# Recurrent attention and a feed-forward block on one core: second products held back, scores of a unit in one run over four PSUM banks, longer table phases

## The chip, the cores and the metric

The kernel runs on one core of a Trainium2 chip. The metric is the device time of one execution in microseconds (us). Before the change the median of 12 runs is 187.29 us (186.58 to 189.39).

## The reference

Only what is computed matters here:

```python
# q, k, v, f_logit: (4, 8, 768, 48)   (batch, heads, time, head width)
f = 1 / (1 + exp(-f_logit))
for t in range(S):
    state = f[:, :, t, :, None] * state + einsum('bhd,bhe->bhde', k[:, :, t], v[:, :, t])
    y[:, :, t] = einsum('bhd,bhde->bhe', q[:, :, t], state)
x = y.transpose(0, 2, 1, 3).reshape(3072, 384)
h = x @ w_in                                    # 384 x 2048
out = (0.5 * h * (1 + erf(h / sqrt(2)))) @ w_out   # 2048 x 384
```

The first half is a recurrence with a decay per channel; the second is a feed-forward block with an exact gelu.

## The kernel before, in words

Time is cut into chunks of 128 steps: 4 batches x 6 chunks = 24 chunks, handled as 12 units of two. The recurrence over a chunk becomes matrix products. For a unit, `decays` takes exp and ln of the forget logits on ScalarE (lines 456 and 459), sums the logarithms over time on TensorE (477 to 482 or 472 to 474, "sums"), and takes exp of the sums both ways, rg (487) and gt (489), and of the chunk's whole decay, gl (492, 496). VectorE multiplies k by rg and q by gt into sc (502, called kp and qp); v is cast to bf16 (507). `turn` transposes sc into kq: for units 0 to 4 on TensorE (535) with a copy out of PSUM (541), for units 5 to 11 by a transposing DMA on SP's queue (523). Then come the scores of a chunk, four pairs of heads, two half-height matmuls at a time (638, or 687 for units 0 to 4, whose rows are interleaved, "paired"), which fill two PSUM banks; VectorE masks them (548) into am. The state is carried by a product on TensorE (648, 699), an addition on VectorE (572), a multiplication (574) and two casts (579) on POOL. The output is the sum of an inner product (661, 719, called Y or YI) and one with the state (616, 622, YX), copied to yb (592) and transposed to xT, on TensorE with a copy for units 0 to 2 (608, 611), else by DMA.

`ffn_group` then takes a unit's 256 rows. Eight first products (755), each of six matmuls into one PSUM bank, are each followed by a gelu on ScalarE (765) into gT. For each of the two chunks 16 second products (774), four in an operation, accumulate in one bank; VectorE copies the bank to osb (788) and SP stores it. The words "first products" and "second products" below mean these.

The order is not written by hand. Every operation is put in a list with its engine, a fixed duration, what it reads and writes, its buffers and a priority; `Plan.run` (line 111 on) places them one after another by a small list scheduler: the operation that can start earliest on its engine, rounded to 0.05 us, then the lowest priority. The instructions are issued in that order, so every engine's order is fixed when the program is built. Exp with ln and gelu live in different tables of ScalarE. When the next operation needs the other table, its start is put off by up to `PATIENCE`; the table load itself is written at line 816. Filler matmuls (811) keep TensorE at work in the first 30 us. Banks are pooled: in `BANKS` five belong to first and second products (`s_fh`), three to attention (`s_m`, `s_ap`).

The order of the loads is the list `LOADS`: u0 stands for the four tensors of unit 0 (f_logit, k, q, v, in the kernel fl, kt, qt, vt), i0 to i2 for the pieces of w_in (win; 1024, 512 and 512 columns), o0 to o3 for those of w_out (wout). Inputs go through SP's queue, weights through POOL's, with a cast. Where the list changes from one queue to the other, a load waits for an earlier one of the other queue (function `load`).

```python
x = max(t, min(t + 2 * TABLE, max([d.vis for d in o.deps] + [switched]) + PATIENCE))
key = (int((x - (EAGER if o.eng == "PE" and o.prio < 900 else 0.0)) * 20 + 0.999), o.prio, o.seq)
```

Of the kernel before, what the change touches and what calls it, by code (L numbers as in the profile page):

```python
# [10 lines left out]
BF16 = mybir.dt.bfloat16  # L11
# [5 lines left out]
LAT = {"PE": 0.25, "ACT": 0.16, "DVE": 0.14, "POOL": 0.12, "DMA": 1.0}  # L17
TABLE = 1.28

PATIENCE = 1.0  # L20

SHARED = 0.5

TURN = 0.1

SPREAD, SEED = (0.0, 0)

EAGER = 0.0
PRI = {'C': 0, 'T': 1, 'A': 2, 'S': 2.5, 'Y': 3, 'X': 4, 'F': 5}
BANKS = (5, 0, 3)  # L30


class Slots:
# [34 lines left out]

class Op:
    __slots__ = ("eng", "dur", "fn", "bufs", "prio", "deps", "table", "start", "end", "vis", "seq", "name",  # L70
                 "left", "outs", "inst", "chain", "opens", "lag", "lat", "port", "mode")


class Plan:
# [3 lines left out]
    def __init__(self):  # L78
        self.ops, self.w, self.r = [], {}, {}

    def add(self, eng, dur, fn, rd=(), wr=(), bufs=(), prio=0.0, deps=(), table=None, name="", chain=None, opens=None, lag=0.0, lat=None, port=False, mode=0):
        o = Op()
        o.eng, o.dur, o.fn, o.bufs, o.prio, o.table, o.name = eng, dur, fn, tuple(bufs), prio, table, name
        o.start = o.end = o.vis = o.inst = None
        o.chain, o.opens, o.lag, o.port, o.mode = chain, opens, lag, port or eng == "POOL", mode
        o.lat = LAT[eng] if lat is None else lat
        o.seq = len(self.ops)
        d = list(deps) + ([chain] if chain else [])
        for k in rd:
            d += self.w.get(k, [])  # L90
        for k in wr:
            d += self.w.get(k, []) + self.r.get(k, [])
        for k in rd:
            self.r.setdefault(k, []).append(o)
        for k in wr:
            self.w[k] = [o]
            self.r[k] = []
        o.deps = list({id(x): x for x in d if x is not o}.values())
        for b in o.bufs:
            b.users.append(o)  # L100
        self.ops.append(o)
        return o

    def run(self):
# [6 lines left out]
        act, switched, mode = None, 0.0, 0  # L111
# [9 lines left out]
        while ready:  # L121
            best = None
            for o in ready:
                t = free[o.eng]
                for d in o.deps:
                    v = d.end if d.eng == o.eng and (o.eng != "DMA" or d is o.chain) else d.vis + o.lag
                    t = v if v > t else t
                ok, taken = True, {}
                for b in o.bufs:
                    if b.slot is None:  # L130
                        v, k = b.slots.free(), taken.get(id(b.slots), 0)
                        if len(v) <= k:
                            ok = False
                            break
                        t = max(t, v[k][0])
                        taken[id(b.slots)] = k + 1
                if not ok:
                    continue
                x = t
                if o.table and act and o.table != act:  # L140
                    x = max(t, min(t + 2 * TABLE, max([d.vis for d in o.deps] + [switched]) + PATIENCE))
                key = (int((x - (EAGER if o.eng == "PE" and o.prio < 900 else 0.0)) * 20 + 0.999), o.prio, o.seq)
                if best is None or key < best[0]:
                    best = (key, t, o)
            if best is None:
                raise RuntimeError("no operation can be placed: %s" % [o.name for o in ready[:20]])
            _, t, o = best
            d = o.dur
            if o.eng == "PE" and o.mode != mode:
                mode = o.mode  # L150
                d += TURN
            if o.port:
                other = port["POOL" if o.eng == "DVE" else "DVE"]
                d += SHARED * max(0.0, min(other[1], t + d) - max(other[0], t))
            if o.table and o.table != act:
                act, switched = o.table, t
# [12 lines left out]
            for n in o.outs:  # L169
                n.left -= 1  # L170
                if not n.left:
                    ready.append(n)
# [17 lines left out]
SIZES = [2, 2, 2, 2, 2, 2, 2, 2, 2, 2, 2, 2]  # L190
PAIRS = [0, 1, 2, 3, 4]
WIN = [1024, 512, 512]
EG = [1]
ET = [0, 1]
EX = [0]
EA = [0, 1]
SPLIT = []
HVC = [0, 1]
HKQ = [0, 2, 4]
HYB = [1]  # L200
HX = []
GKP, GQP = ([], [])
GAM = []
ODVE = [0, 1, 2, 3, 4, 5, 6, 7, 8, 9, 10, 11, 12, 13, 14, 15, 16, 17, 18, 19, 20, 21, 22, 23]
XDMA = [3, 4, 5, 6, 7, 8, 9, 10, 11]
KDMA = [5, 6, 7, 8, 9, 10, 11]
WARM = 30.0
LOADS = ['u0', 'u1', 'i0', 'i1', 'i2', 'o0', 'o1', 'u2', 'o2', 'o3']
LOADS += [f"u{n}" for n in range(12) if f"u{n}" not in LOADS and f"c{2 * n}" not in LOADS]


@with_exitstack
def kernel(
# [59 lines left out]
    s_yb = slots(3, [C, 2, HD], BF16, "yb")  # L273
    s_os = slots(4, [C, d_model], F32, "osb")
    s_xT = {s: slots({1: 4, 2: 4}.get(s, 2), [C, s, KO, C], BF16, f"xT{s}") for s in set(SIZES)}
    s_gT = {s: slots({1: 4, 2: 4}.get(s, 2), [C, FO, s * C], BF16, f"gT{s}") for s in set(SIZES)}
    banks = [pp.tile([C, 512], F32, name=f"ps{i}") for i in range(8)]
    nf, na, _ = BANKS
    s_fh, s_m = Slots(nf, banks[:nf]), Slots(8 - nf - na, banks[nf + na:])
# [115 lines left out]
    wo_src = moe_w_out.rearrange("(r p j) m -> r p j m", r=4, j=4)  # L395
    for what in LOADS:
        m = int(what[1:])
        if what[0] in "uc":
            js = (0, 1)
            if what[0] == "c":  # L400
                js, m = (m % 2,), m // 2
            x = U[m]
            names = (("fl", f_logit), ("kt", k), ("qt", q), ("vt", v))
            if x["pair"]:
                assert what[0] == "u"
                for nm, a in names:
                    if nm == "fl" and m in SPLIT:
                        for i in range(2):
                            load("sp", lambda x=x, a=a, m=m, i=i: nc.sync.dma_start(
                                out=x["fl"].t().rearrange("p (h x) -> p h x", h=H)[:, 4 * i:4 * i + 4], in_=srcp(a, m)[:, 4 * i:4 * i + 4]),  # L410
                                [("fl", 2 * m + i)], [x[nm]], 0.85, f"fl{m}.{i}")
                        continue
# [3 lines left out]
            else:  # L416
                for j in js:
                    for nm, a in names:
                        load("sp", lambda x=x, nm=nm, a=a, m=m, j=j: nc.sync.dma_start(
                            out=half(m, x[nm], j), in_=src(a, 2 * m + j)),  # L420
                            [(nm, 2 * m + j)], [x[nm]], 1.05, f"{nm}{m}.{j}")
        elif what[0] == "i" and m < len(WIN):
            load("pool", lambda m=m: nc.gpsimd.dma_start(out=win[m], in_=win_src[:, :, wcol[m]:wcol[m] + WIN[m]]),
                 [f"win{m}"], [], {512: 2.56, 1024: 4.4}[WIN[m]], what)
        elif what[0] == "o":
            load("pool", lambda m=m: nc.gpsimd.dma_start(out=wout[m], in_=wo_src[m]), [f"wout{m}"], [], 2.15, what)

# [197 lines left out]
    def attn_nat(u):  # L625
        kq = s_kq.new()
        turn(u, kq)
        for j in range(2):
            n = 2 * u + j
            c, x, pr = n % nC, X[n], 10 * n  # L630
            sc, vb = x["sc"], x["vb"]
            aps, ams = [s_ap.new(), s_ap.new()], [s_am.new(), s_am.new()]

            def amm(j=j, aps=aps):
                for p in range(P2):
                    for hh in range(2):
                        r = slice(64 * hh, 64 * hh + 64)
                        nc.tensor.matmul(aps[hh].t()[:, p * C:(p + 1) * C], kq.t()[r, 0, p, j, :], kq.t()[r, 1, p, j, :],  # L638
                                         start=True, stop=True)
            P.add("PE", 0.23, amm, mode=1, rd=[("kq", n)], wr=[("ap", n)], bufs=[kq] + aps + ams, prio=pr + PRI["A"], opens=aps[0], name=f"A{n}")  # L640
            mask_scores(aps, ams, ("am", n), f"AM{n}", ("ap", n), pr, mask, "mask")
            osb = St.get("sb") if c else None
            if c < nC - 1:
                sp = s_m.new()
# [24 lines left out]
    def attn_pair(u):  # L669
# [4 lines left out]
        pr = 10 * n0  # L674
        vbs, scs = [X[n]["vb"] for n in ns], [X[n]["sc"] for n in ns]
        sps = [s_m.new(), s_m.new()] if (n0 + 1) % nC < nC - 1 else [s_m.new()]
        ams = []
        for jk in range(2):
            aps = [(s_fh if jk and u in EA else s_ap).new() for _ in range(2)]
            ams.append([s_am.new(), s_am.new()])  # L680
# [1 line left out]
            def amm(jk=jk, aps=aps):  # L682
                for p in range(P2):
                    for cc in range(2):
                        for hh in range(2):
                            r, t = slice(64 * hh, 64 * hh + 64), slice(64 * cc, 64 * cc + 64)
                            nc.tensor.matmul(aps[hh].t()[t, p * C:(p + 1) * C].rearrange("a (j t) -> a j t", j=2),  # L687
                                             kq.t()[r, 0, p, jk, t], kq.t()[r, 1, p, :, t], start=True, stop=True)
            P.add("PE", 0.35, amm, mode=1, rd=[("kq", n) for n in ns], wr=[("ap", u, jk)], bufs=[kq] + aps + ams[-1],
                  prio=pr + PRI["A"], opens=aps[0], name=f"A{u}.{jk}")  # L690
            mask_scores(aps, ams[-1], ("am", u, jk), f"AM{u}.{jk}", ("ap", u, jk), pr,
# [44 lines left out]
    def ffn_group(g):  # L736
# [31 lines left out]
        for s_ in range(s):  # L768
            op, osb = s_fh.new(), s_os.new()
            n = first[g] + s_  # L770
            for r in range(4):
                def f2(s_=s_, r=r, op=op):
                    for fo in range(4 * r, 4 * r + 4):
                        nc.tensor.matmul(op.t()[:, 0:d_model], gT.t()[:, fo, s_ * C:(s_ + 1) * C], wout[fo // 4][:, fo % 4, :],  # L774
                                         start=(fo == 0), stop=(fo == FO - 1))
                P.add("PE", 0.65, f2, rd=[("gT", g, fo // pk) for fo in range(4 * r, 4 * r + 4)] + [f"wout{r}"],
                      wr=[("o", n)], bufs=[op, gT], prio=pr + PRI["F"] + s_, name=f"F2.{n}.{r}")
            if n == NCH - 1:
                for i, eng in enumerate(("ACT", "DVE")):
                    h = slice(i * d_model // 2, (i + 1) * d_model // 2)  # L780
# [69 lines left out]
```

## Time and profile before

| what | value |
|---|---|
| median of 12 runs | 187.29 us |
| time of the profiled execution | 187.21 us |
| its span, first to last instruction | 185.4 us |
| granted TensorE clock | 1.000 |
| first products, L755 | 576 matmuls, starting at 20.3 us |
| second products, L774 | 384 matmuls |
| gelu, L765 | 96, 671 ns each, 57.2 us busy |
| table loads on ScalarE, L816 and L287 | 27 and 1, 1283 ns each |
| masks on VectorE, L548 | 48, 0.68 us each |
| transfers: HBM read, written | 25.17 MB, 4.72 MB |

How to read it. The profile counts each engine's busy time, but matmuls are pipelined and overlap, so that TensorE's busy time is above its real use; what it costs is read from the starts of successive matmuls in the timeline. The chain of work that ended last follows the execution backwards, from each instruction to what released it. PE is TensorE, PEld its weight loads, DVE is VectorE, ACT ScalarE, POOL GpSimd, SP the engine that issues most transfers; L755 is line 755 of the kernel. In the rows of groups, "x96 | 57.2, 671" means 96 instructions, 57.2 us busy, 671 ns each, and after the next bar stands the idle time of the engine ahead of them. In a timeline the columns are start, length, engine, line, operation and count. In a table by stretch each engine has busy time and, in brackets, its instructions; then come the granted clock (1.00 is full), the DMA share and GB/s.

VectorE's timeline says that it is busy 9.90 of the 10 us from 44 to 54. ScalarE loads the table of gelu for the first time at 18.39 us, and its first gelu starts at 21.15.

### The profile page before, as it was taken

To read this page: it belongs to the slowest core of one execution; us is meant where nothing else is said; L and a number is where in the kernel's file an instruction comes from. 1 tells how busy PE (TensorE), PEld (TensorE's weight loads), DVE (VectorE), ACT (ScalarE), POOL (GpSimd) and SP (SyncE) were. 2 spreads that over 40 slices of the span, in tenths; PEclk is the share of its full clock that TensorE was granted. 3 is DMA by queue.
4 is the path that set the end of the run, shared out by engine and by line. 5 is a ranking of instruction groups with operands and counts; after the bars stand their busy time and mean duration, and the time that the engine had idled before them with its cause. 6 is when DMAs were issued, how large, how long until landed. Compare 5 with 4: busy or idle time off the path is not lost.

```text
span 185.4 us, 5054 instructions
## 1 busy us (share of the span) xinstructions
PE 174.8 (94%) x2054; PEld 135.8 (73%) x2054; DVE 99.9 (54%) x190; ACT 139.8 (75%) x224; POOL 50.6 (27%) x112
## 2 busy tenths in 40 slices
PE   7787999699989999999999998999999999999992
PEld 7565897566668668869778677688687696886960
DVE  4379830029998689086197662573776341622110
ACT  2787677996669989949989979969898389570720
POOL 7338800303221537214116113106151111200000
PEclk9999999999999999999999999999999999999999
DMA  6999999989999999999899899999999931423102
GB/s 150 261 260 153 198 189 274 191 211 238 281 246 205 176 165 221 170 204 242 169 210 220 172 183 166 210 111 250 217 176 211 171 93 53 82 63 85 46 2 83
DMA packets 106422, 32.50 MB, mean 175 GB/s; under 512 B 101536, under 2 KB 105504, under 8 KB 106400
## 3 DMA queue, kind: packets, MB, share of 16 engines
q1 hardware_dynamic: 104480, 28.94, 78.5%
q0 software_dynamic: 1776, 3.15, 10.2%
q8 instruction: 16, 0.26, 0.6%
q10 hardware_dynamic: 144, 0.10, 0.2%
q14 instruction: 6, 0.05, 0.1%
HBM read 25.17 MB, written 4.72 MB: 161 GB/s over the span
## 4 chain that ended last, share of the span: by engine, by line
PE 70%; DVE 10%; DMA 9%; ACT 6%; issue 3%; SPq 0%; DVEq 0%
PE ps L774 29%; PE ps L755 28%; DMA kq<-sc 5%; DMA fl<-in_f_logit_dram 4%; DVE sc L502 4%; PE ps L638 3%; DVE am L548 2%; PE ps L661 2%; ACT L816 1%; ACT lf L459 1%; DVE yb L592 1%; PE ps L535 1%; PE ps L616 1%; PE ps L687 1%; ACT gT L765 1%
## 5 line engine op out<-in xcount | busy, mean ns | idle before, releaser
L755 PE MATMUL ps<-xT,win 128*128 128x256 bf16 x576 | 69.9, 273 | 1.1 <-ACT gT L765 1.1
L765 ACT ACTIVATE gT<-ps 128x512 bf16<-128x512 f32 x96 | 57.2, 671 | 15.3 <-PE ps L755 12.4
L774 PE MATMUL ps<-wout,gT 128*128 128x384 bf16 x384 | 68.3, 326 | 0.0
L755 PEld LDWEIGHTS <-win 128*128 128x128 bf16 x576 | 60.8, 114 | 2.8 <-issue 1.1
L774 PEld LDWEIGHTS <-gT 128*128 128x128 bf16 x384 | 35.7, 98 | 21.3
L816 ACT ACT_TABLE_LOAD x27 | 34.6, 1283 | 0.5
L788 DVE COPY osb<-ps 128x384 f32<-128x384 f32 x23 | 12.7, 554 | 29.1 <-PE ps L774 21.3
L502 DVE TENSOR_TENSOR sc<-kt,rg 128x384 bf16<-128x384 f32 x24 | 15.3, 636 | 21.8 <-ACT rg L487 21.8
L548 DVE TENSOR_TENSOR am<-ps,mask 128x512 bf16<-128x512 f32 x28 | 18.4, 685 | 14.5 <-PE ps L638 14.4
L507 POOL CAST vb<-vt 128x384 bf16<-128x384 f32 x20 | 10.6, 539 | 52.4 <-DMA vt<-in_v_dram 52.2
L574 POOL TENSOR_TENSOR tn<-rr,gl 128x384 f32<-128x384 f32 x16 | 14.0, 875 | 29.5 <-DVE rr L572 12.2
L487 ACT ACTIVATE rg<-ps 128x384 f32<-128x384 f32 x24 | 11.9, 496 | 11.8 <-PE ps L474 6.7
L579 POOL CAST sb<-tn 48x192 bf16<-48x192 f32 x40 | 16.3, 407 | 10.2 <-DVE tn L568 7.2
L592 DVE CAST yb<-ps 128x384 bf16<-128x384 f32 x23 | 12.4, 551 | 8.7 <-PE ps L661 6.9
L456 ACT ACTIVATE fl<-fl 128x768 f32<-128x768 f32 x12 | 10.1, 845 | 7.4 <-DMA fl<-in_f_logit_dram 7.3
L502 DVE TENSOR_TENSOR sc<-qt,gt 128x384 bf16<-128x384 f32 x24 | 15.0, 625 | 0.0
L548 DVE TENSOR_TENSOR am<-ps,maskp 128x512 bf16<-128x512 f32 x20 | 12.7, 682 | 1.7 <-PE ps L687 1.7
L489 ACT ACTIVATE gt<-ps 128x384 f32<-128x384 f32 x24 | 11.9, 498 | 0.0
L459 ACT ACTIVATE lf<-fl 128x768 bf16<-128x768 f32 x12 | 10.1, 844 | 0.3
L572 DVE TENSOR_TENSOR rr<-ps,tn 128x384 f32<-128x384 f32 x16 | 8.9, 554 | 2.0 <-POOL tn L574 0.8
L811 PE MATMUL ps<-junk 128*128 128x128 bf16 x94 | 8.6, 263 | 1.0 <-POOL junk L805 1.0
L811 PEld LDWEIGHTS <-junk 128*128 128x128 bf16 x94 | 7.6, 122 | 1.1 <-POOL junk L805 1.0
(64 smaller groups left out, 124.6 us busy)
## 6 DMA issues: line engine op xcount, KB each, us to landing
out_dram<-osb SPq DMA_DIRECT2D x23, 192.0 KB, 2.6
fl<-in_f_logit_dram SPq DMA_DIRECT2D x14, 192.0 KB, 3.7
kt<-in_k_dram SPq DMA_DIRECT2D x14, 192.0 KB, 3.9
qt<-in_q_dram SPq DMA_DIRECT2D x14, 192.0 KB, 3.5
vt<-in_v_dram SPq DMA_DIRECT2D x14, 192.0 KB, 3.7
fl<-in_f_logit_dram SPq DMA_DIRECT2D x5, 384.0 KB, 5.2
kt<-in_k_dram SPq DMA_DIRECT2D x5, 384.0 KB, 5.7
qt<-in_q_dram SPq DMA_DIRECT2D x5, 384.0 KB, 5.8
```

The source lines that it names most:

```text
L459: P.add("ACT", d, lambda view=view, lo=lo, hi=hi: nc.scalar.activation(lf.t()[:, :, lo:hi, 0:D], view(), AF.Ln, bias=1.0), rd=[("e", u, i) ...
L502: P.add("POOL" if pl else "DVE", 0.80 if pl else 0.475, lambda w=w, a=a, b=b, y=y, j=j, pl=pl: (nc.gpsimd if pl else nc.vector).tensor_tensor(
L548: P.add("POOL" if pl else "DVE", 1.15 if pl else 0.61, lambda hh=hh, pl=pl: (nc.gpsimd if pl else nc.vector).tensor_tensor(ams[hh].t(), ap ...
L574: P.add("POOL", 0.83, lambda: nc.gpsimd.tensor_tensor(tn.t(), rr.t(), glb(), ALU.mult), rd=[("rr", n), ("gl", n)], wr=[("tn", n)], bufs=[r ...
L579: P.add("POOL", 0.36, lambda hh=hh: nc.gpsimd.tensor_copy(sb.t()[64 * hh:64 * hh + D, :, D * hh:D * hh + D], tn.t()[64 * hh:64 * hh + D, : ...
L592: P.add("ACT" if help_ else "DVE", 0.40 if help_ else 0.475, lambda: copier(help_)(yb.t()[:, i, :], yp.t()[:, 0:HD]), rd=[("yp", n)], wr=[ ...
L755: nc.tensor.matmul(hps.t()[:, i * tok:(i + 1) * tok].rearrange("a (s t) -> a s t", s=s), col(fo)[:, kk, :], xT.t()[:, :, kk, :], start=(kk ...
L765: nc.scalar.activation(to, fr, AF.Gelu)
L774: nc.tensor.matmul(op.t()[:, 0:d_model], gT.t()[:, fo, s_ * C:(s_ + 1) * C], wout[fo // 4][:, fo % 4, :], start=(fo == 0), stop=(fo == FO ...
L788: P.add("DVE" if od else "ACT", 0.475 if od else 0.40, lambda op=op, osb=osb, od=od: copier(not od)(osb.t(), op.t()[:, 0:d_model]), rd=[(" ...
L811: nc.tensor.matmul(o.opens.t()[:, 0:C], junk, junk, start=True, stop=True, skip_group_check=True)
L816: nc.scalar.preload_act_table_set({"exp": "natural_log_exp_and_others", "gelu": "gelu_and_others"}[o.table])
```

## The change

The planner gets a rule for second products: while ScalarE's table is that of gelu, the priority number of a second product is raised by `HOLD` = 25, so that other TensorE operations that could start at the same time go first. `PATIENCE` is 3.0 instead of 1.0. Priorities are shifted by a seeded random amount of up to 1. First and second products have four banks instead of five, attention four instead of three.

For units 2 to 11 (list `AJ`) the scores of both chunks are one operation on TensorE, over four banks, which waits for both chunks' kq; the masks follow.

Some operations change engines: the casts of v of units 0 and 1 go from ScalarE to POOL, the kq copies of chunks 2 and 4 from ScalarE to VectorE, the product kp of chunk 2 and qp of chunk 3 from VectorE to POOL. Scores of units 0 and 1 no longer use banks of the feed-forward half; the sums of unit 0 now do. The load order is finer: single tensors of a unit can be named, f, q, k, v. In `LOADS` unit 2's four tensors now stand next to i0 instead of behind o1, and o2, o3 ahead of unit 3 as before.

In the built program ScalarE has 16 table loads instead of 28; TensorE's first and second products are as many as before, and the scores stand in 12 runs instead of 22.

```diff
-PATIENCE = 1.0
+PATIENCE = 3.0
-SPREAD, SEED = (0.0, 0)
+SPREAD, SEED = (1.0, 78)
+HOLD = 25.0
-BANKS = (5, 0, 3)
+BANKS = (4, 0, 4)
...
-                key = (int((x - (EAGER if o.eng == "PE" and o.prio < 900 else 0.0)) * 20 + 0.999), o.prio, o.seq)
+                pr = o.prio + (HOLD if o.held and act == "gelu" else 0.0)
+                key = (int((x - (EAGER if o.eng == "PE" and o.prio < 900 else 0.0)) * 20 + 0.999), pr, o.seq)
...
-EG = [1]
+EG = [0, 1]
-EA = [0, 1]
+EA = []
-HVC = [0, 1]
-HKQ = [0, 2, 4]
+HVC = []
+HKQ = [0]
-GKP, GQP = ([], [])
+GKP, GQP = ([2], [3])
+AJ = [2, 3, 4, 5, 6, 7, 8, 9, 10, 11]
-LOADS = ['u0', 'u1', 'i0', 'i1', 'i2', 'o0', 'o1', 'u2', 'o2', 'o3']
+LOADS = ['f0', 'q0', 'k0', 'f1', 'v0', 'v1', 'k1', 'q1', 'i0', 'k2', 'f2', 'v2', 'q2', 'i1', 'i2', 'o0', 'o1', 'o2', 'o3', 'q3', 'f3', 'k3', 'v3', 'u4']
...
+            if u in AJ:
+                both.append((n, amm, aps, ams))
+                if j:
+                    P.add("PE", 0.46, lambda both=tuple(both): [b[1]() for b in both], mode=1, rd=[("kq", n - 1), ("kq", n)],
+                          wr=[("ap", n - 1), ("ap", n)], bufs=[kq] + sum([b[2] + b[3] for b in both], []), prio=pr - 10 + PRI["A"],
+                          opens=aps[0], name=f"A{n}")
+                    for m, _, a, b in both:
+                        mask_scores(a, b, ("am", m), f"AM{m}", ("ap", m), 10 * m, mask, "mask")
+                continue
...
-                      wr=[("o", n)], bufs=[op, gT], prio=pr + PRI["F"] + s_, name=f"F2.{n}.{r}")
+                      wr=[("o", n)], bufs=[op, gT], prio=pr + PRI["F"] + s_, held=True, name=f"F2.{n}.{r}")
```

The paired units 2 to 4 get the same joint operation in `attn_pair`, with a planned duration of 0.70.

More of the change, by code (lines that the diff above doesn't have):

```diff
@@ L70 @@
     __slots__ = ("eng", "dur", "fn", "bufs", "prio", "deps", "table", "start", "end", "vis", "seq", "name",
-                 "left", "outs", "inst", "chain", "opens", "lag", "lat", "port", "mode")
+                 "left", "outs", "inst", "chain", "opens", "lag", "lat", "port", "mode", "held")
 class Plan:
@@ L79, in __init__, with add @@
         self.ops, self.w, self.r = [], {}, {}
-    def add(self, eng, dur, fn, rd=(), wr=(), bufs=(), prio=0.0, deps=(), table=None, name="", chain=None, opens=None, lag=0.0, lat=None, port=False, mode=0):
+    def add(self, eng, dur, fn, rd=(), wr=(), bufs=(), prio=0.0, deps=(), table=None, name="", chain=None, opens=None, lag=0.0, lat=None, port=False, mode=0, held=False):
         o = Op()
@@ L86, in add @@
         o.lat = LAT[eng] if lat is None else lat
+        o.held = held
         o.seq = len(self.ops)
@@ L206 @@
 KDMA = [5, 6, 7, 8, 9, 10, 11]
+AJ = [2, 3, 4, 5, 6, 7, 8, 9, 10, 11]
+NGT = 4
 WARM = 30.0
-LOADS = ['u0', 'u1', 'i0', 'i1', 'i2', 'o0', 'o1', 'u2', 'o2', 'o3']
-LOADS += [f"u{n}" for n in range(12) if f"u{n}" not in LOADS and f"c{2 * n}" not in LOADS]
+LOADS = ['f0', 'q0', 'k0', 'f1', 'v0', 'v1', 'k1', 'q1', 'i0', 'k2', 'f2', 'v2', 'q2', 'i1', 'i2', 'o0', 'o1', 'o2', 'o3', 'q3', 'f3', 'k3', 'v3', 'u4']
+LOADS += [f"u{n}" for n in range(12) if f"u{n}" not in LOADS and f"c{2 * n}" not in LOADS and f"f{n}" not in LOADS]
 @with_exitstack
@@ L275 @@
     s_xT = {s: slots({1: 4, 2: 4}.get(s, 2), [C, s, KO, C], BF16, f"xT{s}") for s in set(SIZES)}
-    s_gT = {s: slots({1: 4, 2: 4}.get(s, 2), [C, FO, s * C], BF16, f"gT{s}") for s in set(SIZES)}
+    s_gT = {s: slots({1: 4, 2: NGT}.get(s, 2), [C, FO, s * C], BF16, f"gT{s}") for s in set(SIZES)}
     banks = [pp.tile([C, 512], F32, name=f"ps{i}") for i in range(8)]
@@ L397 @@
         m = int(what[1:])
-        if what[0] in "uc":
+        if what[0] in "ucfkqv":
             js = (0, 1)
@@ L404 @@
             if x["pair"]:
-                assert what[0] == "u"
+                assert what[0] != "c"
                 for nm, a in names:
+                    if what[0] not in ("u", nm[0]):
+                        continue
                     if nm == "fl" and m in SPLIT:
@@ L418 @@
                     for nm, a in names:
+                        if what[0] not in ("u", "c", nm[0]):
+                            continue
                         load("sp", lambda x=x, nm=nm, a=a, m=m, j=j: nc.sync.dma_start(
@@ L421 @@
                             [(nm, 2 * m + j)], [x[nm]], 1.05, f"{nm}{m}.{j}")
-        elif what[0] == "i" and m < len(WIN):
+        elif what[0] == "i":
             load("pool", lambda m=m: nc.gpsimd.dma_start(out=win[m], in_=win_src[:, :, wcol[m]:wcol[m] + WIN[m]]),
-                 [f"win{m}"], [], {512: 2.56, 1024: 4.4}[WIN[m]], what)
+                 [f"win{m}"], [], {512: 1.97, 1024: 3.95}[WIN[m]] + (0.5 if order[-1][0] == "sp" else 0.0), what)
         elif what[0] == "o":
@@ L627, in attn_nat @@
         turn(u, kq)
+        both, amss = [], []
         for j in range(2):
             n = 2 * u + j
-            c, x, pr = n % nC, X[n], 10 * n
-            sc, vb = x["sc"], x["vb"]
+            pr = 10 * n
             aps, ams = [s_ap.new(), s_ap.new()], [s_am.new(), s_am.new()]
+            amss.append(ams)
             def amm(j=j, aps=aps):
@@ L639, in amm @@
                                          start=True, stop=True)
+            if u in AJ:
[6 more added lines that the diff above has]
+                        mask_scores(a, b, ("am", m), f"AM{m}", ("ap", m), 10 * m, mask, "mask")
+                continue
             P.add("PE", 0.23, amm, mode=1, rd=[("kq", n)], wr=[("ap", n)], bufs=[kq] + aps + ams, prio=pr + PRI["A"], opens=aps[0], name=f"A{n}")
             mask_scores(aps, ams, ("am", n), f"AM{n}", ("ap", n), pr, mask, "mask")
+        for j in range(2):
+            n = 2 * u + j
+            c, x, pr = n % nC, X[n], 10 * n
+            sc, vb, ams = x["sc"], x["vb"], amss[j]
             osb = St.get("sb") if c else None
@@ L676, in attn_pair @@
         sps = [s_m.new(), s_m.new()] if (n0 + 1) % nC < nC - 1 else [s_m.new()]
-        ams = []
+        ams, both = [], []
         for jk in range(2):
@@ L688, in amm @@
                                              kq.t()[r, 0, p, jk, t], kq.t()[r, 1, p, :, t], start=True, stop=True)
+            if u in AJ:
+                both.append((jk, amm, aps, ams[-1]))
+                if jk:
+                    P.add("PE", 0.70, lambda: [b[1]() for b in both], mode=1, rd=[("kq", n) for n in ns],
+                          wr=[("ap", u, 0), ("ap", u, 1)], bufs=[kq] + sum([b[2] + b[3] for b in both], []),
+                          prio=pr + PRI["A"], opens=aps[0], name=f"A{u}")
+                    for m, _, a, b in both:
+                        mask_scores(a, b, ("am", u, m), f"AM{u}.{m}", ("ap", u, m), pr,
+                                    maskp[:, m].rearrange("a j t -> a (j t)"), "maskp")
+                continue
             P.add("PE", 0.35, amm, mode=1, rd=[("kq", n) for n in ns], wr=[("ap", u, jk)], bufs=[kq] + aps + ams[-1],
```

## The prediction, made before the result was known

> **What bounds the kernel now.** I read the page's busy rows first, then the chain, then TensorE's timeline. The first row of the page calls everybody busy:
>
> ```profile
> PE 174.8 (94%) x2054; PEld 135.8 (73%) x2054; DVE 99.9 (54%) x190; ACT 139.8 (75%) x224; POOL 50.6 (27%) x112
> ```
>
> The chain that ended last says whose work sets the end:
>
> ```profile
> PE 70%; DVE 10%; DMA 9%; ACT 6%; issue 3%; SPq 0%; DVEq 0%
> PE ps L774 29%; PE ps L755 28%; DMA kq<-sc 5%; DMA fl<-in_f_logit_dram 4%; DVE sc L502 4%; PE ps L638 3%; DVE am L548 2%; PE ps L661 2%; ACT L816 1%; ACT lf L459 1%; DVE yb L592 1%; PE ps L535 1%; PE ps L616 1%; PE ps L687 1%; ACT gT L765 1%
> ```
>
> 57% is the two big products of the feed-forward half (L755 "first", L774 "second"), and table loads (L816) only 1%. Busy time by stretch (a modelled sum, so only its shape counts):
>
> ```profile
> core 0: us, PE busy (x) PEld busy (x) DVE busy (x) ACT busy (x) POOL busy (x), PEclk, DMA share, GB/s
> 0.00:20.27 20.27, 16.62 (x293) 13.62 (x293) 13.39 (x35) 13.31 (x23) 11.76 (x39) 1.00 1.05 205
> 20.27:36.41 16.14, 14.48 (x166) 12.54 (x167) 4.39 (x9) 12.81 (x17) 5.02 (x11) 1.00 1.12 215
> 36.41:53.46 17.05, 16.07 (x210) 10.88 (x210) 12.54 (x24) 12.19 (x22) 3.15 (x6) 1.00 1.01 252
> 53.46:181.90 128.44, 127.59 (x1392) 98.80 (x1388) 69.22 (x123) 101.20 (x162) 30.69 (x58) 1.00 0.85 159
> ```
>
> So there is a head of 20.3 us before the first first-product, bound by loads and the first two units of attention; a ragged part to 53.46, where the third group's first products start; and 128.4 us in which TensorE is short of nothing. By starts of successive matmuls in its timeline, that last part has only three gaps, 0.2 us at 72.8, 0.9 at 113.8 and 0.25 at 128.2, 1.3 together: 127.1 of work. Between 20.27 and 53.46 the gaps are 0.8 (33.5), 1.2 (35.2), 0.5 (44.7), 0.7 (50.9) and 0.3 (51.9). Only work taken off TensorE, or these 5 us, can be gained after the head.
>
> **Part 1: scores in one run.** Scores use half the rows of the array. Each run of them pays on entering and on leaving:
>
> ```profile
> 97.05 1.48 PE L755 MATMUL ps<-xT,win 128*128 128x256 bf16 x12
> 98.46 0.40 PE L638 MATMUL ps<-kq 64*128 64x128 bf16 x8
> 98.79 1.50 PE L755 MATMUL ps<-xT,win 128*128 128x256 bf16 x12
> 100.22 0.40 PE L638 MATMUL ps<-kq 64*128 64x128 bf16 x8
> ```
>
> From 98.46 to 98.79 is 0.33 for eight matmuls of 128 columns, two at a time, which stream in 4 x 0.053 = 0.21; the 12 after them need 1.43 instead of 12 x 0.109 = 1.31. A turn there and back costs 0.24. The built order has 22 score runs before and 12 after. Ten fewer: 2.4 us off TensorE, 9 of them (2.2) after the third group starts. This has no cover: it is on the bound. The price is that the run waits for the later of two transposes (rivals).
>
> **Part 2: fewer table loads.** The built order has 16 table loads instead of 28.
>
> ```profile
> L816 ACT ACT_TABLE_LOAD x27 | 34.6, 1283 | 0.5
> ```
>
> 12 x 1.283 = 15.4 us of ScalarE. The Trainium skill (ScalarE: Activation LUTs, What ACT_TABLE_LOAD costs) puts a switch at about 2.66 us, a drain of 1.38 behind the load, and (Rules for kernel authors) has one group by table set. By the page that is 32 us; but the row shows 0.5 us idle before all 27 loads, and neighbours start at once: no drain here, so 15.4. By either, none of it reaches the end in the last 128 us, because TensorE does not wait for ScalarE there. I book 0, where second products cover; without that cover each load would cost 1.28.
>
> **Part 3: held second products.** They are reordered, same number (384), same cost. They must cover ScalarE's exp phases. A late phase is two loads 2.57, exp and ln 1.7, rg, gt and gl of two chunks 2.0: 6.3 us; the order has 28 to 64 second products there (4.6 to 10.4 us) plus attention and first products into free banks. Covered. First products now have four banks: one takes 6 x 0.109 = 0.65, its gelu 0.62 (0.70 in the paired units), so the burst still runs at TensorE's pace.
>
> **Part 4: the loads and the head.** The SP queue now carries k2, f2, v2, q2 (third unit) straight behind the first eight loads, without the wait for weights that f2 had. Before, each 384 KB load took 1.5 us (262 GB/s), the eighth was under way when win0 was issued:
>
> ```profile
> 12.45 2.49 POOL L423 DMA_DIRECT2D win<-in_moe_w_in_dram  x3 [6.17 <-DMA kt<-in_k_dram]
> ```
>
> win0 landed at 20.22. After, it is again issued near 12.5 (the same wait for the sixth load; two casts of 0.54 before it are over by 11.8) and starts moving near 14.5, where SP still has 0.87 MB up to and with f2 (3.3 us) and 0.79 MB of v2, q2 (3.0 us). win0's 0.79 MB take 4.3 us at the 182 GB/s of the window 15 to 20. SP first: f2 17.9, win0 25.1. Even shares: f2 21.2, win0 23. win0 first: win0 19 to 20, f2 22.2. The skill (DMA: Bandwidth & Descriptors, Queues, rings and completion order) says that an engine takes packets from its queues in turn; queue 0's are 3.15 MB / 1776 = 1.8 KB on average, queue 1's 28.94 MB / 104480 = 0.28 KB, so turns favour win0. The trace shows one hint: the eighth load landed 2.5 us after the seventh instead of 1.5 when win0 joined. I take f2 22.2 and win0 by 20.5, and keep 25.1 as the other end. That rule speaks against putting f2 behind the weights.
>
> ScalarE runs f2's exp and ln before the first gelu: 22.2 + 0.85 + 0.85 + 1.28 = 25.2 (21.15 before). Attention of the second unit ends near 20.6 (qp of chunk 3 on POOL to 18.7, transposes 0.25, copy 0.7, scores 0.65), so first products start then, fill four banks, and YI, YX, transposes and sums (2.2 us) fill the wait. The 16th first product follows the 12th gelu: 25.2 + 12 x 0.70 + 0.25 + 0.65 = 34.5. win1 and win2 are issued from 22.2 (f2's landing, and POOL's chain with two more products of 0.88, ends then too) and land near 27 and 30, in time; wout's four follow to 38, in step with their readers.
>
> From 34.5 to the third group TensorE has 64 second products (10.4) and 7.4 of attention: 17.8. One wait: eight transposes of chunk 4 stand behind 24 second products (38.4), but 16 gelus end at 36.4, a load at 37.7, rg and gt at 38.6, products on VectorE at 39.4: 0.8. VectorE was 99% busy from 44 to 54 and takes two kq copies from ScalarE (0.7 each, one here): 0.7 more. Third group at 34.5 + 17.8 + 0.8 + 0.7 = 53.8, against 53.46: what the longer gelu burst and the second products put off win is given back here. What ScalarE no longer casts and copies is worth nothing there. The other bank choices and six more filler matmuls move no work: 0 (they lie in head gaps).
>
> **Sum.** The state at that point is the old one of 53.46 with the fourth unit's state sums and four transposes more done (0.9). Left: 127.1 - 0.9 - 2.2 = 124.0. Waits: 1.3 before, I take 0.9. End of TensorE 53.8 + 124.0 + 0.9 = 178.7 instead of 181.90, 3.2 less; the last copies and store stay. The profiled execution took 187.21 with a span of 185.4; it lies at the median of 187.29. 187.2 - 3.2 = 184.0.
>
> **Rivals.**
> 1. Turns are saved and waits eat some of it. A joint run waits for both transposes: from the sums (Cn) to it needs ScalarE 2.0, VectorE 1.3, a transpose 3.3 at the median and 5.3 at worst, 6.6 to 8.6; the order gives 7.5 to 9.1. If most take 5, up to 1 us in three of seven units, 2.2 with the smaller slips: 186.2. For it: the 0.9 gap at 113.8 followed such a transpose (5.3). Against: 10 transposes after 90 us have a median of 3.3, and the old cover there was shorter (6.1). Chance 0.17.
> 2. Slower: SP's queue goes first at 14.5. win0 lands at 25.1, TensorE stands from 20.6 but for six filler matmuls; the skill (TensorE: Matmul & The Clock Gate, Part 1) lets the clock fall to half after an idle window of about 3.4 us, until 3.4 us of work have passed: 1.7 lost. No run here shows it (PEclk 1.00 throughout). Then 12.7 of work (96 first products 10.5, 2.2 attention): 39.5; + 17.8 + 0.5 = 57.8; + 124.9 = 182.7, 0.8 later than 181.90; with SP's later loads slipping a little too, 188.2. It decides from win0 landing at about 24.3. Against: the eighth load's delay. Chance 0.20.
> 3. It does not do what it says: excluded for the order (16 loads, joint runs, 64 held products stand in it).
>
> Likeliest case (as summed, 181.8 to 186): 0.63. A change of less than 0.3% (0.56 us) can't be told from none. Faster 0.71 (the first case, and most of rival 1), same 0.08, slower 0.21. The range reaches from all gaps closed (3.2 + 2.2 more: 181.8) to rival 2: 181.8 to 188.3.
>
> **What would show it.** Right: about 15 table loads at L850; score runs of 16 at 0.66 from start to next; first gelu near 25, third group's first product near 54, TensorE end near 178.7. Wrong: win0 after 24; gaps ahead of score runs released by a kq transpose; PEclk below 9 near 25; gaps above 1 us ahead of transposes while ScalarE finishes gelus.

## The result, and the profile after

The changed kernel has a median of 185.46 us (184.32 to 186.68, 12 runs), beside 187.36 for the kernel before (49 runs); the ratio is 0.990, with a 95% interval of 0.988 to 0.992. It is 1.0% faster; 1.8% was forecast (184.0), inside the range of 181.8 to 188.3. Ratios are formed from the faster of the two states in which a kernel runs, so that they can differ a little from the quotient of two medians.

The profiled execution of the changed kernel took 184.32 us, with a span of 182.3; it is the shortest of its runs, where that of before lay at the median. The two traces are 3.1 us apart, the medians 1.9. The first row of the page, the chain that ended last, and the group of table loads (count, busy time, mean ns, idle time ahead of them):

```profile
PE 172.1 (94%) x2060; PEld 136.6 (75%) x2060; DVE 100.2 (55%) x190; ACT 121.2 (66%) x206; POOL 53.1 (29%) x118
...
PE 80%; DVE 5%; DMA 3%; POOL 3%; SPq 3%; ACT 3%; issue 1%; POOLq 0%; DVEq 0%
...
L850 ACT ACT_TABLE_LOAD x15 | 19.2, 1283 | 0.3
```

ScalarE lost 18.6 us of busy time, six times the 3.1 us between the two traces. TensorE's share of the chain rose from 70% to 80%: fewer waits stand between its instructions. The table by stretch, cut at the first first-product (before 20.27), at the first second product, at the third group's first products (before 53.46) and at the end of TensorE's work (before 181.90). The second cut has no counterpart in the table of before, so only the sum of the middle rows is compared:

```profile
core 0: us, PE busy (x) PEld busy (x) DVE busy (x) ACT busy (x) POOL busy (x), PEclk, DMA share, GB/s
0.00:21.46 21.46, 16.37 (x286) 13.28 (x286) 13.96 (x36) 9.35 (x17) 14.58 (x45) 1.00 1.10 233
21.46:35.10 13.64, 13.63 (x176) 12.89 (x175) 3.39 (x7) 11.86 (x18) 5.45 (x11) 1.00 1.03 183
35.10:52.38 17.28, 17.28 (x236) 11.69 (x234) 13.83 (x27) 9.91 (x19) 3.14 (x7) 1.00 1.10 259
52.38:178.77 126.39, 124.86 (x1372) 98.79 (x1368) 68.62 (x121) 89.73 (x152) 29.91 (x56) 1.00 0.82 161
```

First products start 1.2 us later (21.46 for 20.27). From there to the third group it takes 30.9 us instead of 33.2, and TensorE is busy all the time in both rows, 0.67 us of it with twelve fillers, for which the kernel before has no counterpart after its first products began:

```profile
26.57 0.83 PE L845 MATMUL ps<-junk 128*128 128x128 bf16 x12
27.24 8.02 PE L789 MATMUL ps<-xT,win 128*128 128x256 bf16 x72
```

From the third group to the end it is 126.4 instead of 128.4. The 3.1 us lie there: +1.2 - 2.3 - 2.0.

A joint score run in TensorE's timeline:

```profile
96.78 1.26 PE L789 MATMUL ps<-xT,win 128*128 128x256 bf16 x10
97.97 0.62 PE L649 MATMUL ps<-kq 64*128 64x128 bf16 x16
98.53 1.72 PE L789 MATMUL ps<-xT,win 128*128 128x256 bf16 x14
```

Sixteen matmuls from 97.97 to 98.53, 0.56, where two runs of eight took 0.33 each and slowed the products behind them twice (prediction, part 1).

To compare kernels I add up TensorE's waits: the times by which one matmul's start to the next exceeds its streaming time by more than 0.2 us, after 24 us. That is 4.8 us before and 2.0 after, 2.7 with the fillers, which stand where TensorE would have waited. So two savings of about equal size meet: 2.1 us of waits, and ten turns, 2.1 us by the first experiment. Less the 1.2 us by which first products start later they make 3.0 of the 3.1 us.

### The profile page after: what moved, and what is told of

It reads as the page before. It is cut to its first block, busy times and chain, and to the rows that moved or that the text cites. A ratio compares the mean times of both kernels' runs of the same rounds, so it can differ in the third digit from the quotient of the medians.

```text
span 182.3 us, 5058 instructions
## 1 busy us (share of the span) xinstructions
PE 172.1 (94%) x2060; PEld 136.6 (75%) x2060; DVE 100.2 (55%) x190; ACT 121.2 (66%) x206; POOL 53.1 (29%) x118
## 4 chain that ended last, share of the span: by engine, by line
PE 80%; DVE 5%; DMA 3%; POOL 3%; SPq 3%; ACT 3%; issue 1%; POOLq 0%; DVEq 0%
PE ps L789 33%; PE ps L808 32%; DMA vt<-in_v_dram 3%; DVE sc L512 3%; SPq L421 3%; PE ps L649 2%; PE ps L685 2%; ACT gT L799 1%; PE ps L545 1%; PE ps L482 1%; PE ps L632 1%; PE ps L626 1%; PE ps L753 1%; POOL sc L512 1%; PE ps L672 1%
## 5 line engine op out<-in xcount | busy, mean ns | idle before, releaser
L799 ACT ACTIVATE gT<-ps 128x512 bf16<-128x512 f32 x96 | 58.0, 670 | 21.0 <-PE ps L789 19.7
L789 PE MATMUL ps<-xT,win 128*128 128x256 bf16 x576 | 69.2, 273 | 0.0
L808 PE MATMUL ps<-wout,gT 128*128 128x384 bf16 x384 | 67.6, 326 | 0.3 <-ACT gT L799 0.3
L808 PEld LDWEIGHTS <-gT 128*128 128x128 bf16 x384 | 36.2, 98 | 21.6 <-ACT gT L799 0.4
L517 POOL CAST vb<-vt 128x384 bf16<-128x384 f32 x24 | 12.3, 525 | 45.3 <-DMA vt<-in_v_dram 45.2
L512 DVE TENSOR_TENSOR sc<-kt,rg 128x384 bf16<-128x384 f32 x23 | 13.7, 598 | 20.7 <-ACT rg L497 15.9
L558 DVE TENSOR_TENSOR am<-ps,mask 128x512 bf16<-128x512 f32 x28 | 17.4, 683 | 12.0 <-PE ps L649 11.6
L589 POOL CAST sb<-tn 48x192 bf16<-48x192 f32 x40 | 15.5, 386 | 17.0 <-DVE tn L578 8.7
L512 DVE TENSOR_TENSOR sc<-qt,gt 128x384 bf16<-128x384 f32 x23 | 15.6, 690 | 1.3 <-ACT gt L499 0.9
L558 DVE TENSOR_TENSOR am<-ps,maskp 128x512 bf16<-128x512 f32 x20 | 12.4, 682 | 1.7 <-PE ps L711 1.6
L545 PE MATMUL ps<-ident,sc 128*128 128x128 bf16 x80 | 7.0, 220 | 3.0 <-POOL sc L512 1.7
```

What stands on the lines that cost most here:

```text
L512: P.add("POOL" if pl else "DVE", 0.80 if pl else 0.475, lambda w=w, a=a, b=b, y=y, j=j, pl=pl: (nc.gpsimd if pl else nc.vector).tensor_tensor(
L517: P.add("ACT" if hv else "POOL", 0.40 if hv else 0.47, lambda y=y, j=j, hv=hv: (nc.scalar.copy if hv else nc.gpsimd.tensor_copy)(y["vb"].t ...
L558: P.add("POOL" if pl else "DVE", 1.15 if pl else 0.61, lambda hh=hh, pl=pl: (nc.gpsimd if pl else nc.vector).tensor_tensor(ams[hh].t(), ap ...
L589: P.add("POOL", 0.36, lambda hh=hh: nc.gpsimd.tensor_copy(sb.t()[64 * hh:64 * hh + D, :, D * hh:D * hh + D], tn.t()[64 * hh:64 * hh + D, : ...
L789: nc.tensor.matmul(hps.t()[:, i * tok:(i + 1) * tok].rearrange("a (s t) -> a s t", s=s), col(fo)[:, kk, :], xT.t()[:, :, kk, :], start=(kk ...
L799: nc.scalar.activation(to, fr, AF.Gelu)
```

## The experiments

My theory when they began: the gain is turns saved on TensorE; table loads are beside the point. The rival: the gain is the long table phases and the held second products. Ratios are to the kernel before on the same chip.

**1 and 2. Ten turns put back, order otherwise kept.** In each joint run, a full-height filler either between the two chunks or, as a control, ahead of both (`first` is True there; the paired units are changed in the same way):

```diff
+    def joint(both, first):
+        for i, b in enumerate(both):
+            if i == (0 if first else 1):
+                nc.tensor.matmul(b[2][0].t()[:, 0:C], junk, junk, start=True, stop=True, skip_group_check=True)
+            b[1]()
...
-                    P.add("PE", 0.46, lambda both=tuple(both): [b[1]() for b in both], mode=1, rd=[("kq", n - 1), ("kq", n)],
+                    P.add("PE", 0.46, lambda both=tuple(both): joint(both, False), mode=1, rd=[("kq", n - 1), ("kq", n)],
```

> The changed kernel with one full-height filler matmul between the two chunks of each of the ten joint score runs: the order is otherwise the same, TensorE pays ten turns there and back more. My theory (the gain is the turns saved, on the bound): 10 x (0.24 + 0.06) = 3.0 us above the changed kernel's 185.46, near 188.4, slower than the kernel before. Rival (the gain comes from the longer table phases and the held products, turns vanish in waits): at most 1 us more, 185.5 to 186.5.

> The same ten filler matmuls, but ahead of each joint run, where the turn is paid anyway: both theories expect only the fillers, 10 x 0.06 = 0.6 us, near 186.0. The difference to the kernel with the filler in the middle is the price of ten turns: 2.4 us by my theory, near 0 by the rival.

Measured: filler in the middle 187.5 us, ratio 0.995 (0.992 to 0.999); control 185.9, ratio 0.988 (0.982 to 0.993); the kernel before ran at 188.8 on this chip. The medians are 1.6 us apart, the spans 2.1 (185.1 and 183.0). The same run in the timelines, filler in the middle first:

```profile
120.74 2.13 PE L795 MATMUL ps<-xT,win 128*128 128x256 bf16 x18
122.80 0.40 PE L655 MATMUL ps<-kq 64*128 64x128 bf16 x8
123.13 0.23 PE L638 MATMUL ps<-junk 128*128 128x128 bf16 x1
123.29 0.40 PE L655 MATMUL ps<-kq 64*128 64x128 bf16 x8
123.62 1.50 PE L795 MATMUL ps<-xT,win 128*128 128x256 bf16 x12
```

And the control:

```profile
119.49 2.13 PE L795 MATMUL ps<-xT,win 128*128 128x256 bf16 x18
121.45 0.22 PE L638 MATMUL ps<-junk 128*128 128x128 bf16 x1
121.61 0.62 PE L655 MATMUL ps<-kq 64*128 64x128 bf16 x16
122.16 1.50 PE L795 MATMUL ps<-xT,win 128*128 128x256 bf16 x12
```

From the first products' start to the ones after the scores it is 2.88 and 2.67: one turn there and back costs 0.21 us (0.24 predicted), ten of them 2.1. The granted clock was half from 16.1 to 19.5 us in the first of these profiles and full there in the second, but that is not the difference: first products start at 21.74 and 21.65, and from there to the end of TensorE's work it is 159.8 and 157.8, 2.0 us apart. This part of the theory is shown: turns are paid in full on the bound.

**3 and 4. No table loads at all.** Exp stands in the place of gelu, so one table serves the whole kernel:

```diff
-nc.scalar.activation(to, fr, AF.Gelu)
+nc.scalar.activation(to, fr, AF.Exp)
...
-                nc.scalar.preload_act_table_set({"exp": ..., "gelu": ...}[o.table])
+                pass
```

> The kernel before with exp in the place of gelu, so that one table serves the whole kernel and all 27 later table loads are left out; the feed-forward half is thus another function. The order of every engine is the same. My theory (loads are covered but for the ragged part): the waits of 0.8 and 1.2 us near 33 to 36 go, and little else: 2.0 to 2.5 us, near 185. Rival (table loads are what the change gained on): 27 loads are 34.6 us of ScalarE, and far more comes back, 4 us or more, below 183.4.

> The changed kernel with exp in the place of gelu and no table load after the first; the feed-forward half is thus another function. My theory: the first gelu starts 1.28 us earlier, the waits of 0.4 near 60 and part of 0.96 near 68 go: 1.5 to 2 us, near 183.7, so that the changed kernel stays 1 to 2 us below the one before, without any table load in either. Rival: with no loads in either, the changed kernel has lost its advantage, and both are equal within 0.5 us.

Measured: the kernel before without 27 loads 0.996 (0.993 to 0.999); the changed one without 15 loads 0.988 (0.985 to 0.992). 34.6 us of ScalarE gave back 0.4% or 0.8 us, less than I expected; the waits of TensorE stayed (5.1 us for 4.8), they only moved to other releasers. In the changed kernel nothing came back that could be told from none. Its profile shows where part may have gone: the wait near 68 us grew from 1.0 to 2.1, because ScalarE waited 1.9 us for a load of f_logit, and the clock was half from 70.9 to 74.3 (last section). Without any load in either, the changed kernel is still ahead by 0.8 points. So the time of the table loads costs almost nothing here, as long as the order is kept; that they go hand in hand with the order is another matter.

**5 to 8. One part alone, one part undone.** Joint runs alone in the kernel before (with the four banks that they need); the changed kernel with single score runs; the changed kernel without holding; and the changed kernel again:

```diff
# 5: the kernel before
-BANKS = (5, 0, 3)
+BANKS = (4, 0, 4)
+AJ = [2, 3, 4, 5, 6, 7, 8, 9, 10, 11]
# 6: the changed kernel
-AJ = [2, 3, 4, 5, 6, 7, 8, 9, 10, 11]
+AJ = []
# 7: the changed kernel
-HOLD = 25.0
+HOLD = 0.0
```

> The kernel before with the joint score runs alone, and the four attention banks that they need (so four for the products): no holding, old patience, old loads, old engines. Its order has 12 score runs and 32 table loads. My theory (turns on the bound are the gain): about the measured price of ten turns, 1.6 to 2.4 us less than the kernel before, ratio 0.987 to 0.992, although it has four table loads more. Rival (longer table phases): no gain or a loss, ratio 1.000 or above.

> The changed kernel with the scores of each chunk on their own again, all else as changed: 21 score runs, 24 table loads. My theory: nine turns come back and the table loads matter little: ratio to the kernel before 0.998 to 1.003. Rival: it keeps holding, patience and loads, so most of the gain stays, ratio 0.990 to 0.994.

> The changed kernel without holding (HOLD 0): 12 score runs, 22 table loads. My theory: six table loads more lie beside TensorE's work and the joint runs stay: ratio to the kernel before 0.989 to 0.993, as the changed kernel. Rival (holding is what keeps TensorE busy in ScalarE's exp phases): TensorE runs dry, 2 us or more above the changed kernel, ratio 1.000.

> The changed kernel again, so that it is timed beside these three on one chip: ratio 0.988 to 0.992 by all theories.

Measured: joint runs alone 1.072 (1.066 to 1.078); single runs 1.031 (1.025 to 1.037); no holding 1.040 (1.034 to 1.046); the changed kernel 0.987 (0.983 to 0.992). My theory failed in the first three, and with it the simple sum: the parts don't add up. The rivals had the sign of kernels 5 and 7, but nowhere near the size, and kernel 6 lies above both expectations. TensorE's waits are 15.3 us with joint runs alone, 7.8 with single runs, 11.8 without holding. The chain of the kernel with joint runs alone:

```profile
PE 44%; ACT 33%; DVE 7%; DMA 6%; issue 4%; SPq 3%; POOL 1%; DVEq 0%; POOLq 0%; ACTq 0%
PE ps L789 19%; PE ps L808 18%; ACT L850 13%; ACT gT L799 10%; DMA fl<-in_f_logit_dram 4%; SPq L429 3%; DVE sc L512 3%; ACT fl L466 3%; ACT rg L497 3%; DVE am L558 3%; ACT lf L469 2%; DMA vt<-in_v_dram 2%; ACT gt L499 1%; PE ps L685 1%; PE ps L649 1%
```

Here table loads, 1% of the chain before, are 13%. The waits are 10.5 us more than before, ten turns fewer save 2.1, and the span is 14.5 us longer. The rest fits the clock, which was half from 36.8 to 40.2 and from 60.7 to 70.9 us: 13.6 us at half clock cost up to 6.8 (an estimate, for a TensorE that works all the time).

Without holding, TensorE's waits are these (total, times, longest):

```profile
PE ps L789 <- ACT gT L799: 4.9, 4, 1.9
PE ps L672 <- DVE sc L512: 2.3, 3, 0.9
PE ps L482 <- ACT lf L469: 1.7, 2, 1.3
```

The longest of them, in TensorE's timeline:

```profile
129.02 1.48 PE L789 MATMUL ps<-xT,win 128*128 128x256 bf16 x12
130.34 0.33 PE L672 MATMUL ps<-vb,sc 128*128 128x96 bf16 x4
132.60 1.47 PE L789 MATMUL ps<-xT,win 128*128 128x256 bf16 x12 [1.94 <-ACT gT L799]
```

and what ScalarE did meanwhile:

```profile
128.93 0.50 ACT L497 ACTIVATE rg<-ps 128x384 f32<-128x384 f32 x1 [2.02 <-PE ps L484]
...
130.66 1.28 ACT L850 ACT_TABLE_LOAD   x1
131.96 2.56 ACT L799 ACTIVATE gT<-ps 128x512 bf16<-128x512 f32 x5
```

TensorE has no second product left (224 have started by 129.0, all those of the seven units whose first products had ended), fills the banks it has with first products, and stands until the exps, the load and the first gelu are over. From a gelu to the next one behind a phase of exps, this kernel has two phases, near 99 and 146 us, with no second product at all; the changed kernel has 16 to 58 in every phase after 30 us. So holding takes no work off TensorE; it is the cover without which the changed kernel, with its joint runs and four banks for products, loses far more than the turns it saves. How much of that is the lost bank was not measured: no kernel here changes the banks alone.

**9 to 11. Is it the draw of the order, or the rule?** The scheduler reacts to every edit, so that an undone part also draws a new order. Three more, 9 and 11 from the changed kernel, 10 from the kernel before:

```diff
# 9
-BANKS = (4, 0, 4)
+BANKS = (5, 0, 3)
-AJ = [2, 3, 4, 5, 6, 7, 8, 9, 10, 11]
+AJ = []
-SPREAD, SEED = (1.0, 78)
+SPREAD, SEED = (1.0, 76)
# 10: 5, and
-PATIENCE = 1.0
+PATIENCE = 3.0
+HOLD = 25.0
# 11
-SPREAD, SEED = (1.0, 78)
+SPREAD, SEED = (1.0, 80)
-HOLD = 25.0
+HOLD = 0.0
```

> The changed kernel without joint score runs, and with five banks for the products and three for attention as before (seed 76): 24 score runs, and 16 table loads as in the changed kernel. If turns are the gain: 12 runs more at 0.16 to 0.24 us each are 1.9 to 2.9 us above the changed kernel, ratio to the kernel before 0.997 to 1.003. If holding and long table phases are the gain: ratio 0.987 to 0.991, as the changed kernel.

> The kernel before with joint runs, four and four banks, holding and patience 3.0, but the old loads and engines: 12 score runs, 14 table loads. If joint runs covered by holding are the gain by themselves: ratio 0.987 to 0.992. If the longer first gelu phase also needs the third unit loaded earlier: the ragged part up to 55 us loses 2 us and the gain is gone, ratio 0.998 to 1.006.

> The changed kernel without holding and with another seed (80): 12 score runs, 20 table loads. If the loss without holding was a bad draw of the order: ratio 1.00 or below. If holding is what covers ScalarE's exp phases when products have only four banks: 1.03 or above, with TensorE waiting for gT again in the late part.

Measured: holding without joint runs, with five banks, 0.995 (0.992 to 0.998), between the two expectations; joint runs with holding but the old loads and engines 1.001 (0.997 to 1.005); no holding with another seed 1.037 (1.031 to 1.043).

Kernel 11 speaks against a bad draw as the cause of the loss without holding: with a second seed the waits are 10.8 us again. Kernel 9 has the 16 table loads of the changed kernel, twice its score runs (24) and the fewest waits of all, 1.3 us: 12 turns x 0.21 = 2.5 us, less 0.7 of waits and less the 0.7 us of fillers that it does not have at 26 us, make 1.1; 0.8 was measured (186.2 against 185.4, on different chips), and 1.4 lies between the two traces from the start of first products to the end of TensorE's work. So half of the gain, 0.5 of 1.0%, is had without a single joint run. Kernels 6 and 9 differ in the banks and in the seed; which of the two makes 3.1% slower into 0.5% faster was not taken apart.

Kernels 5 and 10 differ in holding and `PATIENCE` alone: 1.072 and 1.001, the largest step of all. But kernel 10 has 12 score runs and holding, and gains nothing: its waits are 5.5 us, two of them for gelus,

```profile
PE ps L789 <- ACT gT L799: 2.9, 2, 1.5
PE ps L487 <- ACT lf L469: 1.6, 2, 1.0
```

late ones (the largest near 73 and 100 us), not in the ragged part as I had expected. The 3.5 us more of waits than in the changed kernel eat the 2.1 of the turns. (Beside the kernel before, 2.1 us of turns less 0.7 us of added waits leave 1.4; its trace is 0.5 us shorter, and the rest is open.) Whether the load order, the moved casts and copies or the seed makes the difference to the changed kernel was not taken apart, and `PATIENCE` was never changed alone.

**12. More fillers in the head.** In one of its profiles (kernel 8) the changed kernel's clock fell after 18 us (last section). This version has 30 fillers more ahead of two sets of transposes, where TensorE waits for POOL:

```diff
+            more, bank, lo = {"Tk2": (12, o.opens, 0), "Tq3": (18, o.bufs[0] if o.bufs else None, 256)}.get(o.name, (0, None, 0))
+            for _ in range(more):
+                nc.tensor.matmul(bank.t()[:, lo:lo + C], junk, junk, start=True, stop=True, skip_group_check=True)
```

> The changed kernel with 30 filler matmuls more between 14 and 19 us, where TensorE waits for POOL (12 ahead of the transposes of chunk 2, 18 ahead of the second transposes of chunk 3). If the half clock seen near 18 to 23 us in one profile of the changed kernel comes from the sparse stretch ahead of it: the granted clock stays at 0.995 or above in nearly all runs and the median falls by 0.5 to 1 us, ratio 0.982 to 0.986. If not: clock and time as the changed kernel, 0.987 to 0.991.

Measured: 184.74 us (184.38 to 185.74), ratio 0.987 (0.983 to 0.991), against 185.46 and 185.28 for the changed kernel in its two sets. The granted clock was 0.996 or above in all six runs; in the changed kernel's 18 it was 0.991 or below in ten. The changed kernel was not run on this chip; here the kernel before had 0.991 or below in 10 of 23 runs. The clock did as expected; the gain in time of 0.5 to 0.7 us is within the intervals and not shown. It is the lowest median of all kernels here.

## Why the prediction was right, and where it was not

- **What bounds it**: right. Only TensorE's work and its waits moved the end; leaving out every table load gave back 0.8 us in one kernel and nothing in the other (kernels 3 and 4).
- **Part 1, turns**: right in mechanism, 0.21 us for 0.24, 2.1 for 2.4.
- **Part 2, table loads at 0**: right within 0.8 us for 27 of them. The Trainium skill's 2.66 us per switch (ScalarE: Activation LUTs, What ACT_TABLE_LOAD costs) would have made 72 us of those 27 (an estimate); the trace's 1.283 and its 0.5 us of idle time ahead of 27 loads were the better figures.
- **Part 3, holding at 0 as cover**: the sign and the role were right, but I named its price without cover only as 1.28 us per load and did not follow it up. It is the condition of the whole gain: 4.0% and 3.7% slower than before without it (kernels 7 and 11). Nor was it said that holding closes waits of the kernel before and so gains by itself, which kernel 9 shows for holding, patience, loads and moved work together. That part 1 can't be had alone was missing from the rivals: joint runs alone, with the banks that they need, lose 7.2%.
- **Part 4, the head**: the landing of win0 20.5 predicted, 21.4 in the trace; f2 22.2 and 22.7; the first gelu 25.2 and 25.77; 16 first products of two groups done 34.5 and 35.1. That win0 landed ahead of f2 fits the turns between queues of the Trainium skill (DMA: Bandwidth & Descriptors, Queues, rings and completion order); SP first would have put win0 at 25.1. First products started 0.9 us later than the 20.6 that I said, as win0 landed.
- **The ragged part**: two terms failed, in opposite directions. The third group began at 52.38, not 53.8: the stretch began 0.6 us late, but the waits of 0.8 and 0.7 us in it did not come (second products ended at 39.0, and the transposes followed at once), and its work was 17.3, not 17.8. Later waits were put at 0.9 and are 2.0: 0.6 at 55.4, 0.4 at 60.0 and 1.0 at 67.8. The first was released by VectorE's products (L512), the last by its masks (L558); among the waits of the whole execution:

```profile
PE ps L545 <- DVE sc L512: 1.1, 2, 0.6
PE ps L845 <- POOL junk L839: 1.0, 1, 1.0
PE ps L482 <- DVE am L558: 0.8, 1, 0.8
```

  So VectorE's queue did make TensorE wait, at 55 and 68 us instead of between 44 and 54. TensorE's work from the third group on was 124.4 against 124.0, its end 178.77 against 178.7. That the end agrees so closely is in part luck: the third group was 1.4 early, the waits behind it 1.1 and the work 0.4 too long.
- **The number**: 184.0 matches the profiled execution (184.32) and is 1.5 us below the median of the runs. The weak step is that the sum for one profiled execution was taken over to the median unchanged: the profile of before lay at its median, the one after is the shortest of its runs. Part of this distance may be the clock (last section); but the runs of the changed kernel at 0.996 and above, of both sets, still have a median of 185.2, so that 1.2 us stay unexplained.
- **Rivals**: the first (a joint run waits for the later transpose) did not occur, no such wait is in the trace. The second (SP's loads first) did not occur as told, though its last link, half clock after a sparse head, was met in other profiles of the changed kernel's head, where win0 landed near 21.5.

## What to carry to other kernels

Look for waits before busy time: 34.6 us of table loads off an engine beside the bound gave back 0.8 us, 2.1 us of turns on the bound were paid in full. But a saving on the bound can cost the cover of a neighbour: here the joint runs pay only together with second products kept for the time in which ScalarE can't serve the first. Try such parts together and apart, and where a scheduler redraws the order on every edit, add a test that leaves the order alone.

## What the runs showed of the hardware that was not expected

The granted clock fell to half after stretches shorter and less empty than the idle 3.4 us that I had counted on in rival 2. In the changed kernel without table loads, TensorE stood 1.9 us near 69 us. Stretches of 2 us from 68 on:

```profile
68.00:70.00 2.00, 0.17 (x13) 0.10 (x3) 1.97 (x4) 1.69 (x2) 1.00 (x2) 1.00 0.94 168
70.00:72.00 2.00, 1.97 (x19) 1.55 (x19) 1.33 (x4) 1.24 (x4) 0.00 (x0) 0.71 1.09 221
72.00:74.00 2.00, 2.00 (x47) 1.40 (x47) 0.87 (x2) 1.27 (x4) 0.00 (x0) 0.50 0.85 225
74.00:76.00 2.00, 2.00 (x32) 1.74 (x28) 1.49 (x3) 0.58 (x1) 0.90 (x3) 0.93 0.85 171
```

The clock (after the busy columns) is still full while TensorE stands and is half only when it works again, for 3.4 us. Such a stand does not always do it: behind the 1.94 us of kernel 7, shown above, the clock stayed full.

The same is seen in the head of the changed kernel's second profile (kernel 8), where TensorE was busy 3.5 of 5 us from 15 to 20:

```profile
15.00:20.00 5.00, 3.50 (x52) 2.77 (x53) 3.81 (x8) 0.48 (x1) 4.67 (x9) 0.78 1.16 229
20.00:25.00 5.00, 5.00 (x61) 4.03 (x60) 3.40 (x6) 2.00 (x3) 3.80 (x8) 0.54 0.92 205
```

There 18 first products took 3.17 us instead of 2.15, and the span was 184.3 instead of 182.3. The first profile has the same order, much the same waits, and full clock throughout:

```profile
15.00:20.00 5.00, 3.41 (x58) 2.68 (x59) 4.04 (x8) 0.48 (x1) 4.67 (x9) 1.00 1.16 232
```

So whether the clock falls differs from run to run. But it goes with the kernel's head: of the nine profiles with the changed loads and without the 30 fillers, seven (kernels 1, 4, 6, 7, 8, 9 and 11) have the clock fall to half between 16 and 19 us; of the four with the old loads, none does before 36 us. With the 30 fillers TensorE was busy 4.5 of those 5 us, the clock was full there in the one profile, and the mean clock was 0.996 or above in all six runs. What it is in the head that the clock answers to stays open: it held in the control (kernel 2), where TensorE was busy only 2.95 of those 5 us.
